# An attention and expert kernel: k and q transposed by VectorE in 32x32 blocks instead of by TensorE

## The chip, the cores and the metric

The kernel runs on one core of a Trainium2 chip. The core has five engines that run side by side, each through its own list of instructions in order: PE (TensorE, matrix products and transposes), DVE (VectorE), ACT (ScalarE), POOL (GpSimd) and SP (SyncE, which here only issues DMAs). The profile shows PE's weight loads as an engine of their own, PEld. Data moves between DRAM and the on-chip memory (SBUF) by DMAs; PE writes its results to a second on-chip memory, PSUM. An engine waits for another through semaphores, so a late instruction holds back everything behind it on its engine.

The metric is device time in microseconds (us), less is better.

## The reference

Two parts, one after the other. First an attention without softmax over 8 batches, 12 heads, 448 tokens and 64 columns a head:

```python
scores = scale * np.matmul(q, k.transpose(0, 1, 3, 2)) - np.log(S)
attn = 1.0 / (1.0 + np.exp(-scores))
return np.matmul(attn, v).astype(np.float32)
```

Then its output, as 3584 tokens of 768 columns, goes to 8 experts. Every token is assigned greedily, by its largest gate logit, to an expert that still has room (448 tokens each), and gets `max(x @ w1[e], 0) @ w2[e]`. All inputs and outputs are float32.

## The kernel before, in words

The attention works through 48 pairs of heads, batch by batch, six pairs a batch; a pair fills 128 partitions with the 64 columns of two heads. The routing and the expert products follow it and are not touched by the change.

**Loads.** `load(b, g)` fetches a group of four heads (two pairs): k and q of the group go to the tiles `nk` and `nq`, v to `nv` and `nr`. A partition of `nk` or `nq` holds four tokens; each token's 64 columns are one run of 256 bytes. Partitions 0 to 55 hold one half of the tokens, partitions 64 to 119 the other. That makes eight DMAs a group for k and q (L376), four for `nv` (L379) and two for `nr` (L381), nearly all issued by SP, one group every two pairs, two groups ahead of use. The tiles have two buffers.

**Turn.** The score product needs k and q with the columns on the partitions. `turn(b, pr)` does it for one pair: 16 products with the identity on PE for 56 tokens each, eight for k and eight for q (L407; the profile shows them as 56x128), into two PSUM tiles `tp`. Then every float32 value is split in two: ACT copies `tp` to `kqH` in the rounded type fp32r (L413, two instructions of 128x448), and DVE takes the difference to `kqL` (L414, two of 128x448). `kqH` and `kqL` have three buffers.

**Scores.** `scores(b, pr, c)` makes the score tile of 128 keys by 448 queries, both heads. `products` (L425) adds up three products, KH with QH, KH with QL and KL with QH, for two heads: six matmuls into a PSUM tile `sc`, of which there are three. ACT turns `sc` into `at` with the sigmoid (L437). A pair has tiles c = 0, 1, 2; the last 64 keys of two pairs share the tile c = 3, which only the odd pair makes, from k and q of both pairs.

**Values.** `av(b, pr)` multiplies `at` by v (L450, and L456 for the last 64 keys) into `tp` tiles, and DVE copies the result to `xt` (L458; after an odd pair also L460). `tp` has two buffers, shared by `turn`, `av`, the gate logits (L471) and the transposes of `xt` (L482).

**Order.** The order is written out by hand in the loop over pairs; no scheduler changes it. Iteration i makes the scores of pair i, turns pair i + 1 and multiplies pair i - 1 by v. In an even iteration PE's order is c0, turn, c1, c2, av (with L456); in an odd one c0, c1, turn, c2, c3, av. ACT has the splits of the turn ahead of the sigmoid of c0 in an even iteration, and ahead of that of c1 in an odd one. Two iterations, an even and an odd one, are called a period here; there are 24. Once a batch, in an odd iteration, the gate logits stand before av.

Of the kernel before, what the change touches and what calls it, by code (L numbers as in the profile page):

```python
# [7 lines left out]
F32 = mybir.dt.float32  # L8
# [323 lines left out]
def moe_attention(tc, q, k, v, w_gate, w1, w2, out):  # L332
    nc = tc.nc
# [6 lines left out]
    with contextlib.ExitStack() as ctx:  # L340
# [21 lines left out]

        HALVES = [(slice(64 * h, 64 * h + CP // 2), slice(CP // 2 * h, CP // 2 * h + CP // 2)) for h in range(2)]

        def load(b, g, qq=nc.sync, vq=nc.sync):

            nat["v", b, g] = ld.tile([128, G4, 3, D], F32, name="nv", bufs=3)
            nat["r", b, g] = ld.tile([128, 2, D], F32, name="nr", bufs=3)
            for n in "kq":
                nat[n, b, g] = ld.tile([128, 2, NCH, 2, D], F32, name="n" + n)  # L370
            for i in range(2):
                for n, src in (("k", k), ("q", q)):
                    h0 = g * G4 + 2 * i
                    rws = src[b, h0:h0 + 2].rearrange("h (p c) d -> p c h d", c=NCH)
                    for to, fr in HALVES:
                        (qq if n == "q" else nc.sync).dma_start(nat[n, b, g][to, i], rws[fr])  # L376
# [3 lines left out]
            for i in range(2):  # L380
                vq.dma_start(nat["r", b, g][HI if i == 0 else LO],  # L381
                                  vs[2 * i:2 * i + 2, 384:].rearrange("h p d -> p h d"))
# [13 lines left out]
        def turn(b, pr):  # L396

            g, h0 = (2 * pr) // G4, (2 * pr) % G4  # L400
            TP = [ps_t.tile([128, 512], F32, name="tp") for _ in HALVES]
            HC = CP // 2
            for i, n in enumerate("kq"):
                for c in range(NCH):
                    o = (i * NCH + c) * HC
                    for t, (pp, _) in zip(TP, HALVES):
                        nc.tensor.transpose(t[:, o:o + HC], nat[n, b, g][pp, h0 // 2, c].rearrange("p h d -> p (h d)"),  # L407
                                            ident[pp, pp])
            TH = wk.tile([128, 2, CP, NCH], F32R, name="kqH", bufs=3)
            TL = wk.tile([128, 2, CP, NCH], F32R, name="kqL", bufs=3)  # L410
            for t, (_, cc) in zip(TP, HALVES):
                t = t[:, :S].rearrange("p (n c r) -> p n r c", n=2, c=NCH)
                nc.scalar.activation(TH[:, :, cc], t, AF.Copy)  # L413
                nc.vector.tensor_tensor(TL[:, :, cc], t, TH[:, :, cc].bitcast(F32), OP.subtract)  # L414
# [408 lines left out]
```

## Time and profile before

| | |
|---|---|
| time, median of 3 runs | 935.6 us (932.3 to 935.86) |
| the profiled execution's own time | 937.63 us |
| its span | 935.8 us |
| busy share of the span | PE 95%, PEld 74%, DVE 52%, ACT 49%, POOL 37% |
| attention (pairs), from the timeline | about 4.6 to 320 us of the span |
| instructions on PE of L407, all turns | 768 |

The profile is a page of one execution and a trace that can be asked for more. A row of groups reads: line, engine, operation, output <- inputs, shape, count | busy us, mean ns of one | idle time just before them and what ended most of it. A row of a timeline reads: start, duration, engine, line, operation, operands, count, and in brackets the idle time before it with its releaser. A row of windows gives for a stretch of the span its length, the busy time of PE, PEld, DVE, ACT and POOL with the number of instructions, the granted TensorE clock, the mean busy share of the 16 DMA engines, and the GB/s moved. "SPq" is a DMA being issued by SP; its duration is the time of the issue, not of the transfer. Matmuls are pipelined: a matmul of 448 columns is shown with some 0.37 us, but the next pair of them starts 0.20 us later, so starts are the better measure.

### The profile page before, as it was taken

The page shows a single profiled execution, that of the slowest core. Times are in us where ns is not written, and L with a number is a line of the kernel's source. Part 1 is how long each engine was busy: PE and PEld are TensorE (multiplying, and loading weights), DVE is VectorE, ACT ScalarE, POOL GpSimd, SP SyncE. Part 2 cuts the span into 40 slices and gives each one's busy share as a digit, 9 for nine tenths or more (in the row PEclk, how much of TensorE's full clock was granted, in tenths as well). Part 3 has the DMA queues.
Part 4 walks back from the last instruction along what each step waited for, and adds up shares of the span by engine and source line. Part 5 has one row for each costly group of instructions (what it writes and reads, how often), then busy time and mean ns, then how long its engine had stood idle before and what let it go on. Part 6 is the DMA issues. An engine that isn't in the chain of part 4 may idle for free.

```text
span 935.8 us, 17445 instructions
## 1 busy us (share of the span) xinstructions
PE 888.5 (95%) x6371; PEld 691.9 (74%) x6371; DVE 489.4 (52%) x2053; ACT 459.7 (49%) x681; POOL 348.9 (37%) x258
## 2 busy tenths in 40 slices
PE   6999999999999974999899999999999999999995
PEld 4565656556656442898798897888988888989995
DVE  2433333333333288895877978959869732330110
ACT  5656666666676463343442443444434434443431
POOL 4000000000000001484586495585685683742641
PEclk9999999999999997799899999999999999999998
DMA  6556454454452075443443354254343442642511
GB/s 136 130 125 159 109 118 106 103 114 105 112 118 62 16 253 191 149 136 102 152 134 120 110 161 142 88 160 144 133 143 114 155 151 85 210 127 70 182 46 60
DMA packets 195252, 117.62 MB, mean 126 GB/s; under 512 B 138688, under 2 KB 187840, under 8 KB 195168
## 3 DMA queue, kind: packets, MB, share of 16 engines
q1 hardware_dynamic: 188456, 93.58, 36.9%
q0 software_dynamic: 4864, 22.48, 6.6%
q8 instruction: 50, 0.82, 0.4%
q10 hardware_dynamic: 1848, 0.46, 0.2%
q14 instruction: 34, 0.28, 0.1%
HBM read 94.47 MB, written 22.02 MB: 124 GB/s over the span
## 4 chain that ended last, share of the span: by engine, by line
PE 82%; DVE 10%; issue 4%; POOL 2%; DMA 1%; ACT 0%; SPq 0%; POOLq 0%; DVEq 0%
PE sc L425 14%; PE tp L450 12%; PE sc L689 9%; PE sc L687 9%; PE sc L691 8%; PE sc L724 6%; PE sc L726 6%; PE sc L722 6%; DVE r_junk L170 3%; PE tp L407 3%; PE tp L456 2%; PE tp L652 2%; PE tp L639 2%; PE tp L471 1%; DMA xr<-xs,r_idx 1%
## 5 line engine op out<-in xcount | busy, mean ns | idle before, releaser
L605 POOL TENSOR_TENSOR wl<-wr,wh 128x768 fp32r<-128x768 f32 (+1 forms) x96 | 205.8, 2152 | 136.1 <-ACT wh L603 128.8
L437 ACT ACTIVATE at<-sc,bias 128x896 f32<-128x896 f32 x168 | 158.8, 1019 | 45.6 <-PE sc L425 45.6
L625 POOL DMA_INDIRECT xr<-xs,r_idx x32 | 32.4, 1011 | 370.5 <-DVE r_idx L290 359.7
L726 PE MATMUL sc<-hh,wl 128*128 128x448 f32 (+2 forms) x400 | 151.4, 379 | 0.0
L691 PE MATMUL sc<-xh,wl 128*128 128x448 f32 (+2 forms) x396 | 146.8, 371 | 0.0
L689 PE MATMUL sc<-xl,wh 128*128 128x448 f32 (+2 forms) x396 | 146.5, 370 | 0.0
L724 PE MATMUL sc<-hl,wh 128*128 128x448 f32 (+2 forms) x400 | 145.5, 364 | 0.2 <-POOL hl L699 0.2
L687 PE MATMUL sc<-xh,wh 128*128 128x448 f32 (+2 forms) x396 | 145.5, 367 | 0.0
L722 PE MATMUL sc<-hh,wh 128*128 128x448 f32 (+2 forms) x400 | 143.9, 360 | 0.0
L170 DVE TENSOR_SCALAR_CACHE_REDUCE r_junk<-r_KE,r_T 128x224 bf16<-128x224 f32 x315 | 123.3, 441 | 0.1
L450 PE MATMUL tp<-at,nv 128*64 128x448 f32 x576 | 118.8, 548 | 1.1 <-DVE kqL L414 0.6
L603 ACT ACTIVATE wh<-wr 128x768 fp32r<-128x768 f32 (+1 forms) x112 | 102.0, 939 | 10.3 <-DMA wr<-in_moe_w_dram 10.3
L458 DVE COPY xt<-tp 128x448 f32<-128x448 f32 x48 | 30.0, 625 | 131.0 <-PE tp L456 71.6
L414 DVE TENSOR_TENSOR kqL<-tp,kqH 128x448 fp32r<-128x448 f32 x96 | 55.5, 620 | 72.6 <-ACT kqH L413 72.6
L425 PE MATMUL sc<-kqH 64*128 64x448 f32 (+1 forms) x384 | 86.8, 415 | 1.0 <-ACT kqH L413 1.0
L699 POOL TENSOR_TENSOR hl<-yt,hh 128x896 fp32r<-128x896 f32 x32 | 68.3, 2134 | 45.8 <-ACT yt L698 42.9
L695 ACT ACTIVATE hh<-sc 128x896 fp32r<-128x896 f32 x32 | 29.5, 921 | 111.1 <-PE sc L691 111.1
L450 PEld LDWEIGHTS tp<-at,nv 128*64 128x64 f32 x576 | 37.1, 136 | 60.4 <-issue 46.2
L724 PEld LDWEIGHTS sc<-hl,wh 128*128 128x128 f32 x400 | 75.2, 188 | 7.2 <-issue 1.1
L689 PEld LDWEIGHTS sc<-xl,wh 128*128 128x128 f32 x396 | 75.8, 191 | 6.3 <-issue 0.5
L687 PEld LDWEIGHTS sc<-xh,wh 128*128 128x128 f32 x396 | 76.0, 192 | 5.5
L691 PEld LDWEIGHTS sc<-xh,wl 128*128 128x128 f32 x396 | 76.0, 192 | 4.8
(157 smaller groups left out, 1367.7 us busy)
## 6 DMA issues: line engine op xcount, KB each, us to landing
wr<-in_moe_w_dram SPq DMA_DIRECT2D x64, 384.0 KB
wr<-in_moe_w_dram SPq DMA_DIRECT2D x48, 512.0 KB
nk<-in_k_dram SPq DMA_DIRECT2D x96, 112.0 KB
xs<-xr SPq DMA_DIRECT2D x32, 336.0 KB
nq<-in_q_dram SPq DMA_DIRECT2D x92, 112.0 KB
nv<-in_v_dram SPq DMA_DIRECT2D x92, 96.0 KB
nr<-in_v_dram SPq DMA_DIRECT2D x46, 32.0 KB
xr<-xs,r_idx POOLq DMA_INDIRECT x32, 4.6
```

Source lines behind the costliest of these rows:

```text
L170: nc.vector.tensor_scalar(junk, KE, T[:, i:i + 1].bitcast(F32), None, OP.is_ge, OP.add, accum_out=cnt[:, i:i + 1])
L425: nc.tensor.matmul(p[:m, j, :S], R[half, keys], M[half], start=i == 0, stop=i == 2)
L437: return lambda: nc.scalar.activation(a, p[:, :, :S], AF.Sigmoid, bias=bias, scale=1 / math.sqrt(D))
L450: nc.tensor.matmul(p[j * 64:j * 64 + 64, :S], nat["v", b, g][:, h0 + j, c, :], AT[b, pr, c][:, j, :], start=(c == 0), stop=(c == 2 and pr ...
L603: nc.scalar.activation(hi, raw[u], AF.Copy)
L605: eng.tensor_tensor(lo, raw[u], hi.bitcast(F32), OP.subtract)
L687: nc.tensor.matmul(ph[:, f, lo:hi], wh[:, a, fs], xh[:, dd, lo:hi], start=st, stop=False)
L689: nc.tensor.matmul(ph[:, f, lo:hi], wh[:, a, fs], xl[:, dd, lo:hi], start=False, stop=False)
L691: nc.tensor.matmul(ph[:, f, lo:hi], wl[:, a, fs], xh[:, dd, lo:hi], start=False, stop=en)
L722: nc.tensor.matmul(py[:, d2, :w], wh[:, a, dsl], h1, start=st, stop=False)
L724: nc.tensor.matmul(py[:, d2, :w], wh[:, a, dsl], h2, start=False, stop=False)
L726: nc.tensor.matmul(py[:, d2, :w], wl[:, a, dsl], h1, start=False, stop=(j == 1 and a == 3))
```

## The change

**Loads.** k and q of a pair go to one tile `nkq` (128 partitions, k and q, 928 values) with four buffers. A partition holds 14 whole tokens, one run of 3584 bytes in DRAM: 32 partitions hold a head. Every head is loaded twice, to two groups of 32 partitions; the second copy is shifted by 32 values in the partition, so that at the same place the first group has columns 0 to 31 of a token and the second columns 32 to 63. A DMA fills 32 partitions; a group of four heads now takes 16 DMAs for k and q instead of 8, and twice the bytes.

**Turn.** DVE transposes 32x32 blocks: two instructions a pair (one for k, one for q), each of 14 blocks. Block c takes column run c of 14 tokens apart and writes its 32 tokens at a step of 14 values, so that the tile `kqT` holds the tokens in order. PE has no part in it, and no `tp` tile is used. The split (`split()`) is then one ACT copy of 128x896 and one DVE difference of 128x896, both out of SBUF. `kqH` and `kqL` have two buffers instead of three (the pool's own number).

**Order.** DVE's transposes of pair i + 1 stand at the start of iteration i; the split follows the sigmoid of c0 in every iteration. PE makes c0, c1, c2 (and c3) without anything in between.

```diff
+        NT = S // 32
+        W = NT * D + 32
         def load(b, g, qq=nc.sync, vq=nc.sync):
...
-            for n in "kq":
-                nat[n, b, g] = ld.tile([128, 2, NCH, 2, D], F32, name="n" + n)
             for i in range(2):
-                for n, src in (("k", k), ("q", q)):
-                    h0 = g * G4 + 2 * i
-                    rws = src[b, h0:h0 + 2].rearrange("h (p c) d -> p c h d", c=NCH)
-                    for to, fr in HALVES:
-                        (qq if n == "q" else nc.sync).dma_start(nat[n, b, g][to, i], rws[fr])
+                t = nat["kq", b, 2 * g + i] = ld.tile([128, 2, W], F32, name="nkq", bufs=4)
+                for n, (qn, src) in enumerate(((nc.sync, k), (qq, q))):
+                    for j in range(2):
+                        rws = src[b, g * G4 + 2 * i + j].rearrange("(p c) d -> p (c d)", p=32)
+                        for x in range(2):
+                            o = 64 * j + 32 * x
+                            qn.dma_start(t[o:o + 32, n, 32 - 32 * x:W - 32 * x], rws)
...
         def turn(b, pr):
-            g, h0 = (2 * pr) // G4, (2 * pr) % G4
-            TP = [ps_t.tile([128, 512], F32, name="tp") for _ in HALVES]
-            HC = CP // 2
-            for i, n in enumerate("kq"):
-                for c in range(NCH):
-                    o = (i * NCH + c) * HC
-                    for t, (pp, _) in zip(TP, HALVES):
-                        nc.tensor.transpose(t[:, o:o + HC], nat[n, b, g][pp, h0 // 2, c].rearrange("p h d -> p (h d)"),
-                                            ident[pp, pp])
-            TH = wk.tile([128, 2, CP, NCH], F32R, name="kqH", bufs=3)
-            TL = wk.tile([128, 2, CP, NCH], F32R, name="kqL", bufs=3)
-            for t, (_, cc) in zip(TP, HALVES):
-                t = t[:, :S].rearrange("p (n c r) -> p n r c", n=2, c=NCH)
-                nc.scalar.activation(TH[:, :, cc], t, AF.Copy)
-                nc.vector.tensor_tensor(TL[:, :, cc], t, TH[:, :, cc].bitcast(F32), OP.subtract)
-            KQ[b, pr] = [x[:, i].rearrange("p r c -> p (r c)") for i in range(2) for x in (TH, TL)]
+            T = wk.tile([128, 2, S], F32, name="kqT")
+            for n in range(2):
+                nc.vector.transpose(T[:, n].rearrange("p (r c) -> p c r", c=NT),
+                                    nat["kq", b, pr][:, n, 32:].rearrange("p (c d) -> p c d", d=D)[:, :, :32])
+            H = wk.tile([128, 2, S], F32R, name="kqH")
+            L = wk.tile([128, 2, S], F32R, name="kqL")
+            KQ[b, pr] = [x[:, i] for i in range(2) for x in (H, L)]
+            def split():
+                nc.scalar.activation(H, T, AF.Copy)
+                nc.vector.tensor_tensor(L, T, H.bitcast(F32), OP.subtract)
+            return split
...
-            if cur and cur[1] % 2:
-                scores(*cur, 0)()
-                sig = scores(*cur, 1)
-                if nxt:
-                    turn(*nxt)
-                sig()
-                scores(*cur, 2)()
-                scores(*cur, 3)()
-            elif cur:
-                sig = scores(*cur, 0)
-                turn(*nxt)
-                sig()
-                scores(*cur, 1)()
-                scores(*cur, 2)()
+            split = turn(*nxt) if nxt else None
+            for c in range(4 if cur and cur[1] % 2 else 3 if cur else 0):
+                scores(*cur, c)
+                if c == 0 and split:
+                    split()
```

What moves is seen on two engines. On PE, an even iteration of the steady state, before (c0, the turn of the next pair, c1, c2, then av of the pair before):

```order
L425 MATMUL sc<-kqH 128x448 x2
L425 MATMUL sc<-kqL,kqH 128x448 x2
L425 MATMUL sc<-kqH,kqL 128x448 x2
L407 MATMUL tp<-ident,nk 128x56 x8
L407 MATMUL tp<-ident,nq 128x56 x8
L425 MATMUL sc<-kqH 128x448 x2
L425 MATMUL sc<-kqL,kqH 128x448 x2
L425 MATMUL sc<-kqH,kqL 128x448 x2
L425 MATMUL sc<-kqH 128x448 x2
L425 MATMUL sc<-kqL,kqH 128x448 x2
L425 MATMUL sc<-kqH,kqL 128x448 x2
L450 MATMUL tp<-at,nv 64x448 x6
```

and the same iteration now, with the changed kernel's line numbers (L422 for L425, L447 for L450):

```order
L422 MATMUL sc<-kqH 128x448 x2
L422 MATMUL sc<-kqL,kqH 128x448 x2
L422 MATMUL sc<-kqH,kqL 128x448 x2
L422 MATMUL sc<-kqH 128x448 x2
L422 MATMUL sc<-kqL,kqH 128x448 x2
L422 MATMUL sc<-kqH,kqL 128x448 x2
L422 MATMUL sc<-kqH 128x448 x2
L422 MATMUL sc<-kqL,kqH 128x448 x2
L422 MATMUL sc<-kqH,kqL 128x448 x2
L447 MATMUL tp<-at,nv 64x448 x6
```

The sixteen products with the identity are gone; the rest stands as it stood.

On DVE, two iterations of the steady state (odd, then even), before: `kqL` is the split, `xt` the copy after av.

```order
L414 TENSOR_TENSOR kqL<-tp,kqH 128x2x224 x2
L458 COPY xt<-tp 128x448
L414 TENSOR_TENSOR kqL<-tp,kqH 128x2x224 x2
L458 COPY xt<-tp 128x448
L460 TENSOR_TENSOR xt<-tp,xt 128x448
```

and now (L455 and L457 are the copies, L403 the transposes, L411 the split):

```order
L403 STREAM_TRANSPOSE kqT<-nkq 128x14x32 x2
L411 TENSOR_TENSOR kqL<-kqT,kqH 128x896
L455 COPY xt<-tp 128x448
L403 STREAM_TRANSPOSE kqT<-nkq 128x14x32 x2
L411 TENSOR_TENSOR kqL<-kqT,kqH 128x896
L455 COPY xt<-tp 128x448
L457 TENSOR_TENSOR xt<-tp,xt 128x448
```

The transposes of the next pair stand behind the copies that follow av of the iteration before, and ahead of the split.

More of the change, by code (lines that the diff above doesn't have):

```diff
@@ L436, in scores @@
                 products(p, b, pr, slice(S - 64, S), 64)
[L437 removed]
+            nc.scalar.activation(a, p[:, :, :S], AF.Sigmoid, bias=bias, scale=1 / math.sqrt(D))
         XT = {}
@@ L492, in moe_attention @@
         NPR = len(pairs)
-        turn(*pairs[0])
+        turn(*pairs[0])()
         bg, late = [], []
```

4 lines of the change are left out of this document (1 added, 3 removed).

## The prediction, made before the changed kernel had run

> **What bounds the kernel now.** I read the page first, then the windows and the timeline of a steady stretch of the attention, since only that stage is edited. The page's busy times, and its chain of what ended last by line:
>
> ```profile
> PE 888.5 (95%) x6371; PEld 691.9 (74%) x6371; DVE 489.4 (52%) x2053; ACT 459.7 (49%) x681; POOL 348.9 (37%) x258
> PE sc L425 14%; PE tp L450 12%; PE sc L689 9%; PE sc L687 9%; PE sc L691 8%; PE sc L724 6%; PE sc L726 6%; PE sc L722 6%; DVE r_junk L170 3%; PE tp L407 3%; PE tp L456 2%; PE tp L652 2%; PE tp L639 2%; PE tp L471 1%; DMA xr<-xs,r_idx 1%
> ```
>
> The turn (L407) is in that chain with 3%, some 28 us. Windows of 12.3 us, about one period each:
>
> ```profile
> 123.20:135.50 12.30, 12.30 (x115) 7.26 (x113) 4.09 (x7) 8.32 (x12) 0.00 (x0) 1.00 0.50 114
> 136.90:149.20 12.30, 12.30 (x151) 7.49 (x151) 3.21 (x6) 7.03 (x11) 0.00 (x0) 1.00 0.44 100
> ```
>
> PE is busy all 12.30 us at a granted clock of 1.00; DVE 4.09 and ACT 8.32 of it. The stage is PE's, and ACT is the next engine. One period of the timeline (even iteration from 152.95, odd from 159.01, next even at 165.30, which is av's start at 162.89 and its 2.41):
>
> ```profile
> 152.95 0.47 PE L425 MATMUL sc<-kqH 64*128 64x448 f32 x2
> 153.46 0.37 PE L425 MATMUL sc<-kqH,kqL 64*128 64x448 f32 x2
> 153.67 0.54 PE L407 MATMUL tp<-ident,nk 56*128 56x56 f32 x8
> 154.21 0.45 PE L425 MATMUL sc<-kqH 64*128 64x448 f32 x1
> 155.69 2.48 PE L450 MATMUL tp<-at,nv 128*64 128x448 f32 x12
> 158.10 0.98 PE L456 MATMUL tp<-at,nr 64*64 64x448 f32 x8
> 159.01 0.47 PE L425 MATMUL sc<-kqH 64*128 64x448 f32 x2
> 159.15 0.62 DVE L458 COPY xt<-tp 128x448 f32<-128x448 f32 x1 [2.98 <-PE tp L456]
> 159.69 0.61 DVE L460 TENSOR_TENSOR xt<-tp,xt 128x448 f32<-128x448 f32 x1
> 159.72 0.37 PE L425 MATMUL sc<-kqH 64*128 64x448 f32 x2
> 159.99 1.01 ACT L437 ACTIVATE at<-sc,bias 128x896 f32<-128x896 f32 x1 [1.88 <-PE sc L425]
> 160.13 0.37 PE L425 MATMUL sc<-kqH,kqL 64*128 64x448 f32 x2
> 160.33 0.48 PE L407 MATMUL tp<-ident,nk 56*128 56x56 f32 x8
> 160.82 0.44 PE L425 MATMUL sc<-kqH 64*128 64x448 f32 x1
> 161.04 0.98 ACT L413 ACTIVATE kqH<-tp 128x448 fp32r<-128x448 f32 x2
> 161.51 0.43 PE L425 MATMUL sc<-kqH 64*128 64x448 f32 x2
> 161.91 2.81 ACT L437 ACTIVATE at<-sc,bias 128x896 f32<-128x896 f32 x3
> 162.89 1.35 PE L450 MATMUL tp<-at,nv 128*64 128x448 f32 x6
> ```
>
> **PE's part: what goes.** Without the turn the next score tile would start 0.20 us after the third product of the one before (as 160.13 to 160.33): at 153.66 instead of 154.21, and at 160.33 instead of 160.82. A turn costs 0.55 and 0.49, mean 0.52 us; 47 of them stand in the loop: 47 x 0.52 = **24.4 us**, beside the chain's 28.
>
> **What PE meets next, c3.** In an odd iteration (0 is the start of c0) c1 starts at 0.71, c2 at 1.32, c3 would at 1.93. There are three `sc` tiles, so c3 needs the one of c0, which its sigmoid frees at 161.00 - 159.01 = 1.99; with 0.07 for the hand-over c3 starts at 2.06. The turn stood there and hid this. It costs 0.13 in 24 odd iterations: **+3.1 us**.
>
> **The added wait on ACT.** The split's copy H of the next pair stands ahead of the sigmoids of c1, c2, c3, and PE's next iteration waits for the `sc` tiles these free. With two buffers, H may not be written before c3's first product has read the pair before last: 2.06 + 0.61 + 0.27 (a sigmoid starts 0.27 behind the next tile's start, 159.72 to 159.99) = 2.94. And H needs DVE's transposes, which follow the two copies after av: these end at 160.30, that is 1.29; then two transposes of T each. H starts at max(2.94, 1.34 + 2T). The rows for what follows:
>
> ```profile
> L603 ACT ACTIVATE wh<-wr 128x768 fp32r<-128x768 f32 x64 | 52.7, 847 | 10.3 <-DMA wr<-in_moe_w_dram 10.3
> L603 ACT ACTIVATE wh<-wr 128x1024 fp32r<-128x1024 f32 x48 | 49.3, 1062 | 0.0
> L605 DVE TENSOR_TENSOR wl<-wr,wh 128x768 fp32r<-128x768 f32 x2 | 1.8, 954 | 0.5 <-ACT wh L603 0.5
> L144 DVE TENSOR_TENSOR rt<-ML,rt 112x256 f32<-112x256 f32 x7 | 3.0, 429 | 0.2
> L143 DVE TENSOR_REDUCE rt<-ML 112x32 f32<-112x256 f32 x7 | 4.2, 604 | 0.2
> L192 DVE STREAM_TRANSPOSE r_ct<-r_s 128x32 f32<-128x32 f32 x96 | 20.3, 212 | 3.3
> ```
>
> H of 896 values lies midway between 847 and 1062 ns: 0.95 us, about 0.86 in a row of instructions (two of 0.54 take 0.98 above), against 0.98 today: nothing. Three sigmoids take 2.81. So c3's sigmoid ends 3.67 after H starts. Who waits for it is c2 of the next, even iteration: the odd one takes 6.29 - 0.49 + 0.13 = 5.93 us now, and c2 starts 1.32 later, at 7.25. With 0.07 for the hand-over H must start by 3.51, so **T up to 1.08 us costs nothing, and every 0.1 above it 0.2 us an odd iteration**. In 7 of the 24, where the gate logits give ACT another 1.3 us, it is free; 17 pay. L (954 ns for 768, 1.03 ns a value more from 256 to 768: 1.09 for 896) is ready near 5.4, before 5.93. In an even iteration one copy of 0.63 precedes the transposes, H starts near 2.7 and L ends near 4.8, before its end at 5.51: nothing.
>
> **T itself** is not in the trace at 448 columns. One block of 32 takes 212 ns. Below: 416 more columns at 1.03 give 0.64 us. Above: 14 blocks as 14 instructions, 14 x 0.212 = 2.97. Between lies the step of 14 values in the write. The nearest row is the reduction L143, which reads 256 values at a step of 16: 604 against 429 for a plain instruction of that size, 0.68 ns a value more. 0.64 + 448 x 0.68 = **0.95 us** is what I take, by the row that has the same kind of step: no stall. DVE then has 4 x 0.95 + 2 x 1.09 + 1.86 = 7.8 us in a period of 11.4, fine.
>
> In the Trainium skill, "VectorE: DVE Perf Modes", "The three transpose paths", a 128x128 block on VectorE takes 311 ns; that is a fixed 180 and a column a cycle, and would put T at the lower end. But "Vector Engine (DVE) Microarchitecture Reference", "5.2 Measured stream behaviour on trn2 (trn3 not measured)", speaks against the change: a destination stepping 24 words every element was measured at 2.50 ns a column, which would make T 1.30 us (an estimate from that page). No row here shows a stepped write; see the second rival.
>
> **SP's queue.** Today's issues, each with min/median/max in ns:
>
> ```profile
> L376 SPq DMA_DIRECT2D nk<-in_k_dram x48: 813/842/1471, 103.6 to 247.6; - x48
> L379 SPq DMA_DIRECT2D nv<-in_v_dram x45: 370/488/1482, 99.9 to 239.8; - x45
> L381 SPq DMA_DIRECT2D nr<-in_v_dram x24: 618/646/664, 100.5 to 241.1; - x24
> L489 SPq DMA_DIRECT2D xs<-xr x32: 303/304/945, 75.0 to 360.8; - x32
> ```
>
> A group takes 16 + 4 + 2 issues now, with some 0.045 us between two: 16 x (I + 0.045) + 4 x 0.535 + 2 x 0.695 = 16 I + 4.25 us. A period will have 11.44, with the logits' share 11.9 on average, so I may be 0.475. The new DMA is one run a partition, like `xs`, whose 112 runs take 0.304; the dearer ones have short runs of 256 bytes. I take 0.30 to 0.37: 9.1 to 10.2 us, hidden under PE. The xs stores of the first batch, behind the loads on this queue, are not waited for in the attention.
>
> **The transfers.** 16 x 114,688 bytes and v's 0.46 MB are 2.29 MB a period. The window above moved 114 GB/s at a share of 0.50, so 228 GB/s with all engines busy on 256-byte runs: 10.1 us of 11.9 if long runs go no faster. Hidden, two groups ahead. At the start it isn't: the first pair's eight DMAs (0.92 MB, 4 us) and the second pair's as many come behind each other, where now the first scores start at 8.95:
>
> ```profile
> 4.60 0.32 PE L407 MATMUL tp<-ident,nk 56*128 56x56 f32 x1 [4.60 <-DMA nk<-in_k_dram]
> 8.95 0.74 PE L425 MATMUL sc<-kqH 64*128 64x448 f32 x2 [0.97 <-ACT kqH L413]
> ```
>
> I take **+1 us** there, bounds -1 (first issues are shorter) and +3.
>
> The Trainium skill, "SBUF — State Buffer", "Door 1: The DMA port swizzle", has 189 GB/s for a transfer to 32 partitions, as these reach half the ports: 9.7 + 2.0 = 11.7 us a period by it, just hidden too.
>
> **Sum:** -24.4 + 3.1 + 0 + 0 + 1 = -20.3 us on the profiled execution's 937.6, or 917.3. The median of the runs is 2.0 us (0.2%) below that execution, so 915.3 on its scale: **915 us**. Routing and experts are only earlier.
>
> **The rivals.**
> - *The stepped write costs more than a stepped read.* T between 1.08 and 1.68; for it, that no row shows such a write. With T = 1.30: 0.44 x 17 = 7.5 us back, 923 us; 1.68 gives all 20.3 back. Chance 0.20.
> - *DVE's blocks don't overlap, and DVE decides.* For T over 1.68 the kernel is slower: at 2.3 it pays 2 x 1.22 x 17 = 41 us, 957; at 2.97 DVE's sum is 15.9 us a period against 12.35, 24 x 3.6 = 86 more, 1021. Against it, the 212 of one block exceeds other small instructions by little. Chance 0.10.
> - *SP's issues decide.* For it, `nr` with 64 partitions takes 0.646 with fewer runs than `nv`, so few partitions may be what is dear. I = 0.65: 14.65 us a period against 12.8 now (logits in), 23 x 1.87 = 43, less some 10 of lead: 969; with 0.81, 17.2 us, about 1027. Chance 0.10.
> - *The transfers decide* through the half that 32 partitions reach, with the xs stores beside them: 12.3 us a period, 10 us of gain left, 925. Chance 0.05.
> - *More is gained*, as the c3 wait is hidden and the start is earlier: 909. Chance 0.05.
>
> That the change doesn't do what it says is out: the order has no L407 left.
>
> **How the numbers follow.** The forecast (909 to 921) has 0.50. A measurement of this kernel tells about 0.5% (4.7 us) from no change, so faster is below 930.9: 0.50 + 0.05 + 0.14 of the second case + 0.03 of the transfers = 0.72. Within 0.5%: 0.06 + 0.01 + 0.03 of the case after = 0.10. Slower: 0.07 of DVE, 0.10 of SP, 0.01 of the transfers = 0.18. The range of 8 in 10 is 906 to 945: it leaves out SP's case and the far part of DVE's. The likeliest case's own range is 909 to 921.
>
> **What would show it.** STREAM_TRANSPOSE rows of 128x448 near 0.95 us (0.64 to 1.08 for the forecast); periods of 11.4 us by the starts of c0; short PE waits of c3 on the sigmoid and none of c2; DMA issues of `nkq` near 0.30 to 0.37 us with SP idle at the end of a group; a DMA share under 0.9. I am wrong if T is over 1.08 with PE or PEld waiting on the sigmoid in even iterations, if ACT's copy H waits on DVE far beyond 3.5 us, if `nkq` issues exceed 0.475 us, or if DVE's first transpose of a pair waits for a DMA.

## The result and the profile after

The changed kernel takes 921.65 us (median of 4 runs, 921.06 to 922.3) against 935.44 us (median of 4, 932.3 to 935.86) of the kernel before in the same comparison: a ratio of 0.986, 95% interval 0.9837 to 0.9883. The profiled execution took 921.26 us, its span is 919.5.

The page after, the engines' busy times, the chain of what ended last by line, and the group of the transposes:

```profile
PE 860.3 (94%) x5603; PEld 654.2 (71%) x5603; DVE 565.4 (61%) x2101; ACT 460.5 (50%) x633; POOL 349.2 (38%) x258
PE sc L422 13%; PE tp L447 12%; PE sc L677 8%; PE sc L675 8%; PE sc L679 8%; PE sc L712 6%; PE sc L714 6%; PE sc L710 6%; DVE r_junk L170 3%; PE tp L453 2%; PE tp L640 2%; DMA xr<-xs,r_idx 2%; PE tp L627 2%; DMA nkq<-in_q_dram 1%; POOL wl L
L403 DVE STREAM_TRANSPOSE kqT<-nkq 128x448 f32<-128x448 f32 x96 | 84.9, 959 | 8.7 <-DMA nkq<-in_k_dram 8.6
```

PE has lost 28 us of busy time and DVE has gained 76; the turn's line is gone from the chain, and the new transposes, 959 ns each, are not among the lines shown; the whole chain has 5.4 us of them, all before 83 us of the span. A window of exactly one new period (its length, the busy time of PE, PEld, DVE, ACT and POOL, the granted clock, the DMA share, GB/s):

```profile
146.97:158.17 11.20, 11.20 (x84) 5.86 (x82) 7.32 (x11) 8.42 (x9) 0.00 (x0) 1.00 0.77 208
```

A period takes 11.20 us; the kernel before needed 12.35. PE is busy throughout at a granted clock of 1.00, as before, so the stage is still PE's. DVE is busy for 7.3 us and the DMA share is 0.77. One period of the timeline, an even iteration from 163.29 and an odd one from 168.63 (c0 of each), chosen rows of PE and below them of ACT and of DVE (start, duration, engine, line, operation, operands, count, idle time before it with its releaser):

```profile
163.29 0.47 PE L422 MATMUL sc<-kqH 64*128 64x448 f32 x2
...
164.00 0.37 PE L422 MATMUL sc<-kqH 64*128 64x448 f32 x2
...
165.31 2.48 PE L447 MATMUL tp<-at,nv 128*64 128x448 f32 x12
...
168.63 0.47 PE L422 MATMUL sc<-kqH 64*128 64x448 f32 x2
...
170.35 0.37 PE L422 MATMUL sc<-kqH,kqL 64*128 64x448 f32 x2
170.67 0.47 PE L422 MATMUL sc<-kqH 64*128 64x448 f32 x2
170.97 0.36 PE L422 MATMUL sc<-kqL,kqH 64*128 64x448 f32 x2
...
172.08 0.67 PE L468 MATMUL tp<-xt,wgz 128*32 128x112 f32 x18
166.09 0.95 ACT L410 ACTIVATE kqH<-kqT 128x896 fp32r<-128x896 f32 x1 [0.82 <-DVE kqT L403]
...
169.60 1.01 ACT L434 ACTIVATE at<-sc,bias 128x896 f32<-128x896 f32 x1 [0.76 <-PE sc L422]
163.94 1.76 DVE L403 STREAM_TRANSPOSE kqT<-nkq 128x448 f32<-128x448 f32 x2
...
167.07 1.09 DVE L411 TENSOR_TENSOR kqL<-kqT,kqH 128x896 fp32r<-128x896 f32 x1 [1.36 <-ACT kqH L410]
```

Three things are to be read here. In the even iteration c1 starts 0.71 after c0 (163.29 to 164.00), where the turn made it 1.25 (165.30 to 166.55 below), and from c0 to av it takes 2.02 us; before, the same stretch took 2.74 (165.30 to 168.04). In the odd iteration c3 starts 0.32 after the last product of c2 (170.35 to 170.67) where 0.20 is usual: it waits for the sigmoid of c0, which ran from 169.60 to 170.61. And its second pair of products follows after 0.30 (170.67 to 170.97), not 0.20. The transposes end at 165.70, H starts at 166.09, L ends at 168.16, 0.47 before the next iteration's scores start, whose second product is the first to read it.

The stretch of the kernel before that answers to it:

```profile
165.30 0.47 PE L425 MATMUL sc<-kqH 64*128 64x448 f32 x2
...
166.01 0.54 PE L407 MATMUL tp<-ident,nk 56*128 56x56 f32 x8
...
166.55 0.44 PE L425 MATMUL sc<-kqH 64*128 64x448 f32 x1
166.84 0.43 PE L425 MATMUL sc<-kqL,kqH 64*128 64x448 f32 x2
...
167.66 0.43 PE L425 MATMUL sc<-kqH,kqL 64*128 64x448 f32 x2
168.04 2.48 PE L450 MATMUL tp<-at,nv 128*64 128x448 f32 x12
```

The turn itself is 0.54 (166.01 to 166.55). But the first pair behind it takes 0.29 (to 166.84) where 0.20 is usual, and av starts 0.38 after the last score product, now 0.30. So an even turn cost 0.72 us in all. By the same comparison an odd one cost 0.65: the stretch from c0 to the gate logits went from 3.88 (171.36 to 175.24) to 3.45 (168.63 to 172.08), although 0.22 of waiting came in.

**Where the time went.** The start of the first product with v (L447, before L450) for some pairs, in us; pair p's stands in iteration p + 1:

| pair | before | after |
|---|---|---|
| 0 | 18.12 | 19.65 |
| 2 | 31.10 | 30.85 |
| 4 | 43.44 | 44.34 |
| 10 | 86.25 | 91.11 |
| 46 | 315.75 | 300.40 |

From pair 10 to 46 the changed kernel is 20.2 us shorter. Up to 10 it *loses* 4.9 us, where five periods should have gained 1.15 each. Some of that is the start, 1.5 us. The rest are two places that the prediction does not have:

```profile
30.19 1.14 DVE L103 TENSOR_SCALAR c_kk<-c_t 128x3 int32<-128x3 int32 x15
31.24 1.72 DVE L403 STREAM_TRANSPOSE kqT<-nkq 128x448 f32<-128x448 f32 x2
...
34.97 0.48 PE L422 MATMUL sc<-kqH 64*128 64x448 f32 x2 [1.65 <-ACT at L434]
...
65.04 1.02 DVE L484 COPY xr<-tp 112x384 f32<-112x384 f32 x2
65.65 4.16 PE L447 MATMUL tp<-at,nv 128*64 128x448 f32 x12 [2.23 <-DVE xr L484]
...
76.35 2.48 PE L447 MATMUL tp<-at,nv 128*64 128x448 f32 x12 [1.38 <-DVE xr L484]
...
83.88 2.48 PE L447 MATMUL tp<-at,nv 128*64 128x448 f32 x12 [2.24 <-DVE xr L484]
```

The constants of the routing (L55 to L103) are computed on DVE after iteration 2, from 28.61 to 31.24. The transposes now stand behind them, and PE waits 1.65 us: 2.3 us lost between pairs 2 and 4 against the steady gain of 1.15 a period. Then the tokens' rows of the first batch are transposed by PE into `tp` tiles and copied out by DVE (L484). These copies now stand behind L on DVE, both `tp` tiles stay full, and av waits: 5.8 us in three places by the table of waits. After the first of them av took 4.16 us instead of 2.48. Together 7.4 us are lost between pairs 4 and 10.

### The profile page after: what moved, and what is told of

Same layout as the page of the kernel before. It is cut to its first block, busy times and chain, and to the rows that moved or that the text cites. A ratio compares the mean times of both kernels' runs of the same rounds, so it can differ in the third digit from the quotient of the medians.

```text
span 919.5 us, 16283 instructions
## 1 busy us (share of the span) xinstructions
PE 860.3 (94%) x5603; PEld 654.2 (71%) x5603; DVE 565.4 (61%) x2101; ACT 460.5 (50%) x633; POOL 349.2 (38%) x258
## 4 chain that ended last, share of the span: by engine, by line
PE 77%; DVE 10%; issue 4%; DMA 4%; POOL 3%; ACT 1%; SPq 1%; ACTq 0%; POOLq 0%; DVEq 0%
PE sc L422 13%; PE tp L447 12%; PE sc L677 8%; PE sc L675 8%; PE sc L679 8%; PE sc L712 6%; PE sc L714 6%; PE sc L710 6%; DVE r_junk L170 3%; PE tp L453 2%; PE tp L640 2%; DMA xr<-xs,r_idx 2%; PE tp L627 2%; DMA nkq<-in_q_dram 1%; POOL wl L593 1%
## 5 line engine op out<-in xcount | busy, mean ns | idle before, releaser
L447 PE MATMUL tp<-at,nv 128*64 128x448 f32 x576 | 120.5, 554 | 6.6 <-DVE xr L484 5.8
L422 PE MATMUL sc<-kqH 64*128 64x448 f32 (+1 forms) x384 | 78.8, 407 | 12.7 <-ACT kqH L410 11.1
L403 DVE STREAM_TRANSPOSE kqT<-nkq 128x448 f32<-128x448 f32 x96 | 84.9, 959 | 8.7 <-DMA nkq<-in_k_dram 8.6
L411 DVE TENSOR_TENSOR kqL<-kqT,kqH 128x896 fp32r<-128x896 f32 x48 | 52.4, 1093 | 53.9 <-ACT kqH L410 53.9
L447 PEld LDWEIGHTS tp<-at,nv 128*64 128x64 f32 x576 | 37.5, 138 | 66.4 <-issue 57.8
L593 DVE TENSOR_TENSOR wl<-wr,wh 128x768 fp32r<-128x768 f32 (+1 forms) x16 | 25.1, 1573 | 91.9 <-ACT wh L591 91.9
```

Source lines behind the costliest of these rows:

```text
L422: nc.tensor.matmul(p[:m, j, :S], R[half, keys], M[half], start=i == 0, stop=i == 2)
L447: nc.tensor.matmul(p[j * 64:j * 64 + 64, :S], nat["v", b, g][:, h0 + j, c, :], AT[b, pr, c][:, j, :], start=(c == 0), stop=(c == 2 and pr ...
L593: eng.tensor_tensor(lo, raw[u], hi.bitcast(F32), OP.subtract)
```

## The experiments

The first question was whether those two places are what the changed kernel loses, and then what bounds it without them.

**The first batch's rows early (e1).** The chores (the rows' transposes and the gate logits) are taken right after c0, ahead of the split, so that their DVE copies stand before L.

```diff
                 scores(*cur, c)
+                if c == 0:
+                    for _ in range(2):
+                        if bg:
+                            bg.pop(0)()
                 if c == 0 and split:
                     split()
-            for _ in range(2):
+            for _ in range(0 if cur else 2):
```

> The changed kernel with one edit: the transposes of xt for the first batch (and the gate logits) stand on PE right after c0, and their copies on DVE ahead of the split's difference L instead of behind it. Theory (the copies stand behind L, which waits for H, so the two tp tiles stay held and av waits): the stretch from the fifth to the eleventh av falls from 46.8 to about 39.4 us, the waits of av on DVE's copies go, 914.6 us in all (913 to 916.5). Rival (DVE simply has too much to do in these iterations, wherever the copies stand): 920 to 922.

Measured: 915.86 us (914.05 to 918.01) against 934.41, ratio 0.9794 (0.9762 to 0.9827). From pair 4 to 10 it takes 38.9 us instead of 46.8, and the av of pair 46 starts at 293.71 instead of 300.40 (it is the last but one; the expectations, and the text from here on, call it the last). PE waits for L484 no more. The waits on L484 are the loss, as the theory had it. One thing came in besides: from pair 2 to 4 e1 takes 14.76 us, 1.3 more than the changed kernel, since its stall of 1.65 us there was followed by 3.4 us at a granted clock of 0.5 (35.95 to 39.37), and the changed kernel's was not.

**The same two moves in the kernel before (e4).** The chores early and the constants ahead of the first load, with the turn on PE.

```diff
+        route_consts(nc, cp, K)
         load(0, 0, nc.scalar, nc.gpsimd)
...
+            def chores():
+                for _ in range(2):
+                    if bg:
+                        bg.pop(0)()
             if cur and cur[1] % 2:
                 scores(*cur, 0)()
+                chores()
...
             elif cur:
                 sig = scores(*cur, 0)
+                chores()
                 turn(*nxt)
```

> The kernel before with the same two moves as e2 (PE's transposes of xt and the logits right after c0, constants at the start). Theory (the moves mend what the change broke): the kernel before loses little there, its waits of av on DVE's copies were 1.6 us in all and the constants stood where DVE had time: 932 to 935. Rival (the moves are worth as much without the change): 924 to 927.

Measured: 935.22 us (933.16 to 937.21), ratio 0.9999 (0.9982 to 1.0016), 0.2 above the theory's range and far from the rival's. The moves are worth nothing there, so the two losses belong to the change.

**The constants alone (e9),** in the changed kernel, with the rows left where they were:

```diff
         make_identity(nc, ident)
+        route_consts(nc, cp, K)
         load(0, 0, nc.scalar, nc.gpsimd)
...
-            if i == 2:
-                route_consts(nc, cp, K)
```

> The changed kernel with only the routing constants moved ahead of the first load; the first batch's rows stay where the changed kernel has them. Theory (the constants' 2.6 us on VectorE ahead of a turn lose 2.3 us, and without them the first iterations gain about 1 us at the start besides; the 7.4 us lost behind the copies of the first batch's rows stay; SP stays ahead thanks to that loss): fifth iteration's first second-product near 41, last av 297 to 298.5, time 918 to 920. Rival (without the constants' delay the copies lose more, as the loss is made by a later bound such as SP's loads): 920.5 to 923, no gain.

Measured: 919.95 us (919.21 to 922.11), ratio 0.9836 (0.9806 to 0.9867). From pair 2 to 4 it takes 11.20 (31.81 to 43.01) and not 13.49, so the 2.3 us are the constants'. The interval of its ratio overlaps the changed kernel's (0.9837 to 0.9883), so it is these starts that show the gain and not the time. The gain expected at the start did not come: the first av starts at 20.61, 0.96 later than in the changed kernel. In the eleven profiles of kernels with the change this start lies between 18.4 and 21.5, with no order that I can name, so a term of 1 us there cannot be settled.

**Both moves (e2).**

The edits of e1 and e9 together.

> e1 and, besides, the routing constants are made at the very start, before the first loads, instead of after iteration 2. Theory (2.6 us of small DVE instructions delayed the transposes of one pair, and so H, sigmoids and PE, by 2.3 us; at the start DVE has nothing to do until the first load lands at 7.7 us): another 2.3 to 3.3 us less than e1, 911.3 to 912.3. Rival (the constants only move their cost to the start, as POOL's part delays the v loads or DVE's part the first transposes): 914 to 917.

Measured: 915.04 us (913.53 to 916.28), ratio 0.9784 (0.9755 to 0.9814). This missed. Pair 4's av comes at 41.86, 3.7 earlier than in e1 (2.3 are the constants', 1.3 the half clock that e1 had there), but the last av at 295.07, later than e1's 293.71. The groups of DVE between 95 and 290 us, here and in e1 (L403 is L404 in e2), tell what came in:

```profile
L404 DVE STREAM_TRANSPOSE kqT<-nkq 128x448 f32<-128x448 f32 x66 | 60.8, 964 | 9.3 <-DMA nkq<-in_q_dram 9.0 <-DMA nkq<-in_k_dram 0.2
```

```profile
L403 DVE STREAM_TRANSPOSE kqT<-nkq 128x448 f32<-128x448 f32 x67 | 59.7, 962 | 0.3 <-DMA nkq<-in_q_dram 0.2
```

The transposes wait 9.0 us for q's loads, against 0.2. SP's rows in e2, where a group of loads begins with k (each row is one issue or several behind each other):

```profile
109.54 1.93 SPq L378 DMA_DIRECT2D nkq<-in_k_dram  x4
111.51 1.82 SPq L378 DMA_DIRECT2D nkq<-in_q_dram  x4
...
117.28 1.98 SPq L381 DMA_DIRECT2D nv<-in_v_dram  x4
119.35 1.26 SPq L383 DMA_DIRECT2D nr<-in_v_dram  x2
120.71 2.77 SPq L378 DMA_DIRECT2D nkq<-in_k_dram  x4
...
132.57 2.82 SPq L378 DMA_DIRECT2D nkq<-in_k_dram  x3
```

SP issues without a pause, and these two groups take 11.2 and 11.9 us (109.54, 120.71, 132.57). The other engines need 11.20 and, in every third period, 12.48: 11.63 on average. SP's last issue of `nkq` comes at 283.2 us in the changed kernel and at 283.8 in e2, although e2 is 9.9 us ahead at pair 10. In the changed kernel SP had been given a lead by the very stalls that e1 and e2 take away. The time lies in the rival's range, but not for its reason: the first av starts at 18.78, no later than in e1 (19.65).

**v's loads from POOL (e5).** e2 with `nv` and `nr` issued by POOL, which has nothing to do in the attention; the same bytes.

```diff
-        load(0, 1)
+        load(0, 1, nc.sync, nc.gpsimd)
...
-                    load(nx // 3, nx % 3)
+                    load(nx // 3, nx % 3, nc.sync, nc.gpsimd)
```

> The kernel of e2 (rows early, constants early) with v's loads issued by POOL instead of SP, in the loop and for the second group; POOL has nothing to do in the attention. In e2 the transposes wait 9.0 us between 95 and 290 us for q's DMAs. Theory (SP's issuing sets those waits: 18 issues a group take 11.2 us of a period of 11.2): SP has some 3 us a period to spare, the waits on q's DMAs go to under 1 us in that window, e2's lead at the fifth iteration (41.9 us against e1's 45.6) is kept to the end, last av about 290, and the time is 910 to 912. Rival one (the rows' bytes or the DMA engines themselves are too slow): the waits stay, 914 to 916. Rival two (the 11.2 us period itself was held up by SP): under 907, with a period under 11.0.

Measured: 911.82 us (909.11 to 913.97), ratio 0.9749 (0.9717 to 0.9781), the best kernel of this study. DVE's group and SP's rows in the same places:

```profile
L404 DVE STREAM_TRANSPOSE kqT<-nkq 128x448 f32<-128x448 f32 x66 | 58.1, 956 | 0.0
```

```profile
112.41 1.81 SPq L378 DMA_DIRECT2D nkq<-in_q_dram  x4
116.55 1.70 SPq L378 DMA_DIRECT2D nkq<-in_k_dram  x4
```

The waits are gone, SP has pauses (114.2 to 116.55), and the last av starts at 291.34, as expected (about 290). The period stays at 11.20, so SP did not set it; it only set the stalls. SP's last issue of `nkq` now comes at 264.5 us instead of 283.8, so the same bytes can be carried 19 us sooner, and their rate was not the limit. (The theory counts 18 issues a group; there are 22: 16 for k and q, four for `nv` and two for `nr`.) Whether it is the time of the issues that is relieved or the order of the transfers on SP's queue, this run does not separate; from issue to landing an `nkq` DMA takes 2.7 us at the median in both kernels, which speaks for the issues.

**The same without the two moves (e6):** v's loads from POOL in the changed kernel, nothing else.

> The changed kernel with v's loads issued by POOL and nothing else moved. Theory (in the changed kernel SP is kept ahead by the 7 us that the first batch's copies lose, and the steady period is set by the scores' chain, not by SP): 919 to 922, no difference from 921.7, period 11.2. Rival (SP's issuing holds the period up there too): a period under 11.0 and 913 to 917.

Measured: 930.99 us (928.6 to 933.43), ratio 0.9956 (0.994 to 0.9973): 9 us slower than the changed kernel, which neither theory had. From pair 2 to 4 it takes 21.1 us. Rows of POOL, DVE and PE from the timeline there:

```profile
27.25 3.04 POOL L381 DMA_DIRECT2D nv<-in_v_dram  x4 [11.08 <-PE tp L447]
...
31.49 0.25 POOL L52 IOTA c_ti<- 128x128 int32 x1
...
35.57 0.22 POOL L108 MEMSET c_c<- 128x1 int32 x3
37.98 1.69 DVE L403 STREAM_TRANSPOSE kqT<-nkq 128x448 f32<-128x448 f32 x2
...
41.69 0.74 PE L422 MATMUL sc<-kqH 64*128 64x448 f32 x2 [7.96 <-ACT at L434]
```

POOL's issues wait 11.08 us for a buffer of v (`nv` and `nr` have three, not two), and POOL's part of the routing constants waits behind them; DVE's part waits for POOL's, the transposes for DVE's, and PE for 7.96 us. A queue with room is not free if something that others wait for stands behind the new work. From pair 10 on, this kernel runs as the changed one (209.3 us to pair 46, both), so the theory holds for the steady stretch.

**The price of the turn (e7).** In the kernel before, PE issues the 16 products of each turn twice.

```diff
-            for i, n in enumerate("kq"):
+            for i, n in list(enumerate("kq")) * 2:
```

> The kernel before with TensorE's products of each turn issued twice (the second set writes the same values over the first). It prices what the change takes away from TensorE. The prediction's reading (0.52 us a turn, 47 turns): +24.4, 959 to 961, a period of 13.4 against 12.35. Rival (0.64 us a turn, as the periods of the two traces differ by 1.15 with 0.12 given back): +30, 964 to 967, a period of 13.6. Rival two (the second set is partly hidden or runs at another pace): under 957 or over 970.

Measured: 961.96 us (one run; before on that chip 934.98, and 937.63 for the execution that was profiled). The period is 13.34 against 12.35, so a second set of products costs 0.495 us a turn: nearly the prediction's price for the products, from the period; the time, of one run, is 1 us over its range and 2 under the rival's. The stretch behind the second set takes 1.48 us and behind one set 1.49 (here 179.30 to 180.78, before 166.55 to 168.04):

```profile
178.25 0.54 PE L407 MATMUL tp<-ident,nk 56*128 56x56 f32 x8
...
179.30 0.44 PE L425 MATMUL sc<-kqH 64*128 64x448 f32 x1
179.59 0.42 PE L425 MATMUL sc<-kqL,kqH 64*128 64x448 f32 x2
...
180.78 2.48 PE L450 MATMUL tp<-at,nv 128*64 128x448 f32 x12
```

So the 0.16 to 0.18 us that a turn costs beside its products (0.72 and 0.65 against 0.54 and 0.49) are paid once a turn; they go with the change from one kind of product to another, and not with the number of products.

**Twice the transposes (e3).** In the changed kernel the transposes of even pairs, which run in odd iterations, are issued twice: T is doubled there.

```diff
-            for n in range(2):
+            for n in (0, 1) * (2 - pr % 2):
```

> The changed kernel, in which every transpose of an even pair (they run in odd iterations) is issued twice, so that DVE ends 1.76 us later there. Theory (H starts at the later of 2.94 and 1.34 + 2T; c2 of the next iteration waits when the third sigmoid behind it comes late; today's slack is 0.37 us): 1.76 - 0.37 = 1.4 us in each of 17 odd iterations, nearly none in the 7 with the gate logits, some 3 to 5 us in the first batch: 946 to 951 in one run, with the period at 12.6 us without logits. Rival 1 (DVE has room and PE alone decides): 921 to 923. Rival 2 (the transposes are always on the path): 1.76 x 24 = 42, 962 to 966.

Measured: 947.15 us (one run), period 12.48.

The timeline of one such odd iteration and of c0 of the even one behind it:

```profile
161.80 3.33 DVE L403 STREAM_TRANSPOSE kqT<-nkq 128x448 f32<-128x448 f32 x4
...
165.25 0.95 ACT L410 ACTIVATE kqH<-kqT 128x896 fp32r<-128x896 f32 x1 [2.67 <-DVE kqT L403]
...
167.15 0.47 PE L422 MATMUL sc<-kqH 64*128 64x448 f32 x2 [0.63 <-ACT at L434]
```

The chain that the prediction described is there: H waits for the transposes, the sigmoids wait behind H, and the next, even iteration's scores wait for their tiles. They wait at c0 already (0.63) and again at c1 and c2, where the prediction had c2 alone. It is 1.28 us a period, and nothing where the gate logits stand in the odd iteration, as expected. In the changed kernel H starts 3.09 us after c0 in an odd iteration (168.63 to 171.72), 0.4 before the edge of 3.51 that the prediction gives.

**The step of the write (e8).** The transposes write the tokens of a block one after another. The tokens of k and q then stand in another order than those of v; the work is the same.

```diff
-                nc.vector.transpose(T[:, n].rearrange("p (r c) -> p c r", c=NT),
+                nc.vector.transpose(T[:, n].rearrange("p (c r) -> p c r", c=NT),
```

> The changed kernel with the transposes writing each block's tokens one after another instead of every 14th word; k and q then have their tokens in another order than v and the masks, so the output is another one, the work and the bytes are the same. It prices the stepped write: the transposes of 128x448 took 0.959 us with it. Theory (a step of 14 words costs VectorE about a third; the 128x32 one took 212 ns): 0.60 to 0.70 us each; rival: 0.94 to 0.97, the step is free. Either way H's start is bound by the scores of the pair before and not by the transposes, so the period stays 11.2 and the time is 919 to 922; if the transposes are what H waits for, the period falls by up to 0.6 and the time to 905 to 912.

Measured: 920.67 us (one run), period 11.20.

The group of the transposes (busy us, mean ns of one):

```profile
L403 DVE STREAM_TRANSPOSE kqT<-nkq 128x448 f32<-128x448 f32 x96 | 55.9, 619 | 8.9 <-DMA nkq<-in_k_dram 8.7 <-DMA nkq<-in_q_dram 0.2
```

619 ns instead of 959: the step of 14 values costs 340 ns, 0.76 ns a value. The kernel does not notice. In an odd iteration H starts 3.00 us after c0 instead of 3.09, though the transposes end 0.6 sooner, for now it waits for PE's scores, as the theory had it; in an even one it starts 0.6 sooner, and nothing waits for that.

**Three buffers for H and L (e10),** with three tiles for the rows instead of five, to make room.

```diff
-XA_BUFS = 5
+XA_BUFS = 3
...
-            H = wk.tile([128, 2, S], F32R, name="kqH")
-            L = wk.tile([128, 2, S], F32R, name="kqL")
+            H = wk.tile([128, 2, S], F32R, name="kqH", bufs=3)
+            L = wk.tile([128, 2, S], F32R, name="kqL", bufs=3)
```

> The changed kernel with three buffers for the two rounded parts of k and q, as the kernel before had them, in place of two (to make room the rows' tiles go from five to three). It tells whether the third buffer that the change gave up was worth anything. Theory (with two buffers the rounding starts 0.4 us after the transposes end, and the scores do not wait for it): period 11.20 as before, 920 to 923. Rival (the rounding waits for the scores of two pairs earlier, and so the sigmoid behind it on ScalarE is late and the scores of the fourth chunk wait for it, 0.22 us of every odd iteration): period 10.95 to 11.1 and 914 to 918. A change of the wait on the rows' copies (5.8 us in the changed kernel) belongs to the fewer tiles for rows, not to the buffers.

Measured: 925.11 us (923.33 to 926.23), ratio 0.9886 (0.9856 to 0.9917). From pair 10 to 46 it takes 209.9 us, as with two buffers (209.3); the third buffer is worth nothing. The time is 2 us over the theory's range and 3.5 above the changed kernel's. 1.4 of that is there by the last av, nearly all of it between pairs 2 and 4 (14.80 us against 13.49), where this kernel, like e1, has a stretch of 3.4 us at half clock (36.51 to 39.92). The rest lies behind the last av; it may go with the fewer tiles for the rows, which was not tried apart.

**c3 behind av (e11).** e10 with the product with v taken before c3 in odd iterations, so that c0's sigmoid is long done.

```diff
             for c in range(4 if cur and cur[1] % 2 else 3 if cur else 0):
+                if c == 3:
+                    av(*old)
                 scores(*cur, c)
...
-            if old:
+            if old and not (cur and cur[1] % 2):
                 av(*old)
```

> The kernel of e10 (three buffers for the rounded parts, three for the rows) with one thing moved: in every odd iteration TensorE takes the second products of the pair before ahead of the fourth chunk's scores, not behind them. The fourth chunk then starts 2.5 us later and no longer waits for the sigmoid of the first chunk. Theory (that wait costs 0.22 us in each of 24 odd iterations: 0.12 of waiting, and a first pair of products that takes 0.31 instead of 0.20 after the break): period 10.98 in place of 11.20, 24 times 0.22 is 5.3, so 919 to 921 against e10's 925.1. Rival one (SP's issues, 11.17 us a period, hold the period): 11.15 to 11.20, 924 to 926. Rival two (the third chunk of the even iteration now waits, for the fourth chunk's sigmoid): a period of 11.1 or more, 922 to 926.

Measured: 927.98 us (926.08 to 930.27), ratio 0.9918 (0.9894 to 0.9941), period 11.20. The theory fell. The period and the wait are those of the second rival, the time is 2 us above its range. PE's timeline around a period's joint:

```profile
165.19 0.47 PE L422 MATMUL sc<-kqH 64*128 64x448 f32 x2
...
167.55 0.37 PE L422 MATMUL sc<-kqH,kqL 64*128 64x448 f32 x2
167.84 0.47 PE L422 MATMUL sc<-kqH 64*128 64x448 f32 x2
168.15 0.37 PE L422 MATMUL sc<-kqL,kqH 64*128 64x448 f32 x2
```

c3 starts at 165.19 right behind av. Now c2 of the even iteration (167.84) waits for c3's sigmoid, 0.29 after the product before it, and its second pair comes 0.31 later. With three score tiles the fourth chunk in a row waits here too, though the row begins elsewhere. The extra 3 us against e10 do not come from the steady stretch: between pairs 5 and 11 e11 takes 50.1 us and e10 46.1, with a granted clock of 0.88 against 0.97 from 43 to 98 us.

**All together (e12):** e5 with e11's move and e10's buffers.

> e5 (rows and constants early, v's loads from POOL) with the same move as e11 and its three buffers for the rounded parts and three for the rows. Theory: e5's 911.8, about 1.5 to 3.5 more for the rows' fewer buffers (as e10 has over the changed kernel), 5.3 less for the fourth chunk: 908 to 910, period 10.98. Rival (a new wait in place of the old one): 912 to 916, period 11.1 or more.

Measured: 915.77 us (913.73 to 916.7), ratio 0.9778 (0.9759 to 0.9797), period 11.20: the rival. Of what it loses against e5, 1.4 us are there by c0 of iteration 47 (289.34 against 287.89), since a period with the gate logits takes 12.70 us and not 12.47; the rest lies behind the attention and was not traced further. e5 stays the best.

## Why the prediction was right, and where its steps were off

The forecast was 915 us. The kernel takes 921.65, which lies in the range of 8 in 10 (906 to 945) and 0.65 outside the likeliest case's own (909 to 921). The mechanism of the steady period is the one described. That the sum came so near is partly luck: the turn's price was put 8 us too low and early losses of nearly 10 us were left out. On the profiled execution's scale it was 917.3, and 921.26 was measured:

- **The turn: -24.4 predicted, about -32 measured.** The mis-sized term is the price of a turn: 0.52 us is what its products cost (0.495 by e7), but 0.72 and 0.65 go away with it. What was left out is the slower pair behind the change of products and the later start of av. 47 turns, 24 x 0.72 + 23 x 0.65 = 32.2.
- **c3's wait: +3.1 predicted, 5.3 measured.** The wait itself is 0.12, as predicted (0.13), but the pair behind it then takes 0.30 instead of 0.20: 24 x 0.22. e11's move did not take it away.
- **H, L and the sigmoids: nothing, as predicted.** H was to start at max(2.94, 1.34 + 2T) after c0 and did no harm up to 3.51. It starts at 3.09 (the two transposes together take 1.76), and costs nothing; with a smaller T it starts at 3.00 and nothing is gained (e8), and with twice the T the stall comes in the iteration that was said, though not at c2 alone (e3).
- **T: 0.95 predicted, 0.959 measured;** without the step 0.64 predicted and 0.619 measured. The reduction at a step of 16 values was the right row: 0.68 ns a value, 0.76 here. The rule that spoke against the change, 2.50 ns a column for a destination stepping 24 words ("Vector Engine (DVE) Microarchitecture Reference" of the Trainium skill, "5.2 Measured stream behaviour on trn2 (trn3 not measured)", measured there with another operation), would have given 1.30 us by the prediction's estimate; for this instruction the trace disagrees, since the whole of it takes 0.959.
- **SP's issues: this step was wrong.** I took 0.30 to 0.37 us for an issue and 9.1 to 10.2 us a group, with SP idle at its end. Between 95 and 290 us the changed kernel shows, as min/median/max in ns:

```profile
L378 SPq DMA_DIRECT2D nkq<-in_q_dram x128: 323/420/1462, 99.4 to 283.2; - x128
```

  With the median 0.42 the prediction's own formula, 16 I + 4.25, gives 11.0 us. But seven of the 256 issues take over 1 us, the mean is 0.453, and with the means of v's issues too a group takes 11.6 us: SP has no pause. The limit of 0.475 was not passed, but it was for a period of 11.9 on average, and that came out at 11.63. The price was read from `xs`, whose issues nearly always stand alone: in e5 an `nkq` issue after a pause of more than 0.2 us takes 0.31 us as well, and one right behind another 0.42. It cost the changed kernel nothing only since the early stalls had put the other engines 7 us behind; e2 shows what it costs without them, and e5 that it can be moved.
- **The transfers: hidden, as predicted;** a share of 0.69 from 98 to 300 us.
- **The start: +1 predicted, +1.6 measured** (the first scores start at 10.59 instead of 8.95), within its bounds. What the sum does not have is that iterations 0 and 1 gain only 0.1 and not 1.15: c0 of iteration 2 starts at 22.06, before at 20.52.
- **What was missing: DVE's order in the first ten iterations,** +9.7 us: 2.3 behind the constants and 7.4 behind the first batch's copies. The prediction costed a steady period and said that DVE has room, which is true (7.3 of 11.2 us). It did not ask what else stands on DVE in the stretches that are not steady, now that PE waits for DVE early in an iteration.

Together: -32.2 + 5.3 + 1.6 + 1.1 + 9.7 = -14.5, and 0.6 more because the kernel before lost that itself behind the constants (its av of pair 2 waits 0.57 for L): -15.1. The starts show -15.3 up to c0 of iteration 47 (312.28 before, 296.96 now). Another 1.0 lies behind it, where the change edits nothing, and its cause stays open: -16.37 in all (937.63 to 921.26). The remaining difference to the medians, -13.8, is that the execution profiled before lay 2.2 us above the median of its runs and the one after 0.4 below.

## What to carry to other kernels

When work moves to an idle engine, its instructions join a queue in which other things stand: list what is ahead of them and behind them in the stretches that are not steady (the first iterations, the chores of one batch), not only in the period. A queue that costs nothing because something else is late becomes the next bound when that is mended: here each step of e1, e2 and e5 showed the next. To price work taken out of PE's stream, compare the whole stretch from one fixed event to another, since the products around the removed ones speed up too.

## What the runs showed of the hardware that was not expected

- **The clock after a short stall.** Two windows of the changed kernel around the wait at 65.65:

```profile
62.00:65.60 3.60, 1.42 (x14) 0.86 (x10) 2.52 (x5) 3.07 (x4) 0.00 (x0) 1.00 0.83 242
65.60:69.80 4.20, 4.15 (x16) 1.30 (x17) 0.46 (x1) 0.20 (x1) 0.00 (x0) 0.59 0.84 227
```

  PE was busy for 1.42 of 3.60 us, with no pause longer than 2.23, and then had a mean clock of 0.59 over 4.2 us, which made av 1.68 us longer; before and after, from 58 to 62 and from 69.8 to 74, the clock was 1.00. In the record of the clock it is a half from 65.68 to 69.09, for 3.41 us. "TensorE: Matmul & The Clock Gate" of the Trainium skill, "What's actually happening", has the clock halved after an idle window of some 3.4 us; here a window that was not idle, only sparse, was followed by it. The length of the stall does not decide it alone. The stall of 2.24 us at 83.88, as long as the first, was not followed by a half clock, nor were those of 1.65 at 34.97 and 1.38 at 76.35; in e1 the same stall of 1.65 us at 34.96 was. Where it falls counts: the record's stretches up to 320 us are multiples of 3.41 us, and counted on that grid PE was busy for 1.19 us in the stretch before the half clock (62.26 to 65.68), while the stall at 83.88 lies across two stretches with 2.31 and 2.27. In the traces with the change, a full clock was halved after every stretch with less than 1.4 us of PE and after none with more than 1.9 (up to 317 us); between them both occur (1.76 in e1 was followed, 1.78 in the changed kernel was not).
- **A break in PE's stream costs beyond its length:** the first pair of products after a wait or after another kind of product takes 0.29 to 0.31 us to the next pair, where 0.20 is usual.
- **A DMA issue right behind another costs more than one alone:** one run of 3584 bytes on each of 32 partitions took SP 0.42 us behind another issue and 0.31 after a pause of more than 0.2 us (medians in e5; in the rows shown there, four take 1.81 us at 112.41 and 1.70 at 116.55, behind a pause). The rows' store with 112 partitions, issued alone, took 0.304, so the small number of partitions is not what costs.
